# Copies of x's other half rows and stores issued by SP or ScalarE, some low parts on GpSimd, and new tables of order, banks and engines

## The chip, the cores and the metric

The kernel runs on one core of one Trainium2 chip. The metric is device time in microseconds (us) of one launch; lower is better. The engines are named as in the profile: PE is TensorE (PEld its weight loads), DVE is VectorE, ACT is ScalarE, POOL is GpSimd, SP is SyncE, which in the kernel before issues every DMA. "Banks" are the eight PSUM banks.

## The reference

Attention with 64-wide causal blocks over 8 batches, 8 heads, 576 rows and 64 columns a head, and then a mixing layer on its result. Cut to what matters:

```python
scores = (q @ k.transpose(0, 1, 3, 2)) / 8            # 8 batches, 8 heads, 576 x 576
scores = np.where(pos_i // 64 >= pos_j // 64, scores, -1e9)
attn = softmax(scores)                                # by rows
x = (attn @ v), heads side by side                    # 8 x 576 x 512, float32
theta = x @ w_theta
y = w_tok_r @ (x * cos(theta)) + w_tok_i @ (x * sin(theta))   # over the 576 rows
u = x + y
out = u + maximum(u @ w_ch, 0)
```

The four weights come in float64, the rest in float32.

## The kernel before, in words

**Products in halves.** Most matmuls take float16 operands that come in two: a high part (the value, scaled and rounded) and a low part (what the rounding left). A product is then three matmuls: high by high, low by high, high by low. The high part is made by a copy or a scaling, the low part by `value * scale - high`, which is one instruction on DVE (scalar_tensor_tensor) where a scale is needed. So `q_high`, `q_low`, `k_high`, `k_low`, `v_first`, `v_second` make the parts of a pair's q, k and v (`qh`, `ql`, `kh`, `kl`, `v1`, `v2`), `Weight.high_part` and `Weight.low_part` those of the weights, `high` and `low` those of the exponentials, `z_high` and `z_low` those of x times cosine and sine, `u_high` and `u_low` those of u. The start is different: batches 0 to 2 take q and k in float32, the first eight heads turn their exponentials on PE instead of by DMA, and the first four multiply them with v in float32.

**Attention.** A pair p is two heads. PE writes its scores into banks (`scores_wide`, `scores_narrow`, `scores_first`), DVE takes the largest of each row (`maxima`, tiles m), POOL or DVE makes of it the offset of the exponentials (`bias`, also on m), ACT the exponentials (`exponentials`, tiles t), then come their two parts (tile p) and a transposing DMA (`turn`, tile pt). PE multiplies them with v (`weighted`) into one bank o, and DVE divides by the row sums into the tile xn (`normalise`). The last 64 rows of a pair are spread over both halves of the partitions, so each head ends with a copy of 64 rows of 64 floats from one half of the partitions to the other, a DMA from xn to xn (`other_half`). The two parts of xn (tile xp) are turned by a second transposing DMA (`x_turn`, tile xT).

**Mixing.** PE makes theta from xT (`theta`), ACT and DVE reduce it to a turn between -1/2 and 1/2 (`turns`, `rest`, `size`), ACT makes sine and cosine (`sines`, with a load of ACT's function table ahead and behind), DVE and POOL multiply with x (`times_x`), and PE does the mixing over rows (`mix`) and the channel product (`channel`). ACT or DVE does the maximum (`rectify`), DVE the sum (`total`, into xT's buffer), and a DMA writes 128 x 576 floats of the result (`store`, xT to out, 32 in all).

**Order.** Nothing is scheduled at build time. The program consists of 3,444 parts (`add(key, f, needs, ...)`): `needs` are the parts that must stand earlier. Three tables fix the rest: ORDER is the order in which the parts are recorded, and so the order of each engine's queue; BANKS says which bank each product gets; PLACES names, for each part with an `on=` list, the engine that does it (A is ACT, D is DVE, P is POOL). `emit` walks through them:

```python
    for n in ORDER:
        key = keys[n]
        assert done.issuperset(parts[key].needs), key
        parts[key].f(*([place[key]] if parts[key].on else []))
```

Every engine runs its queue in order, and so does SP with its DMAs: a transfer whose data is late holds back every DMA recorded behind it. A DMA also waits until the one eight DMAs ahead of it has landed, since they share eight semaphores in turn. The two kinds of transfer that the change speaks of are added so:

```python
            add(("half", n), h.other_half, needs)                 # needs: normalise of head n
            part("store", (e,), m.store, [("out", b, e, th) for th in range(2)])
```

Of the kernel before, what the change touches and what calls it, by code (L numbers as in the profile page):

```python
# [21 lines left out]
ALU = mybir.AluOpType  # L22
# [17 lines left out]
    160, 158, 8, 0, 16, 9, 32, 40, 24, 10, 11, 334, 333, 1, 56, 339, 2, 338, 362, 363, 350, 17, 351, 3, 370, 18, 352,  # L40
    371, 48, 19, 33, 4, 353, 372, 20, 360, 41, 361, 335, 42, 354, 373, 12, 340, 336, 337, 364, 162, 374, 34, 382, 164,
    25, 365, 26, 383, 57, 5, 366, 386, 341, 58, 27, 59, 342, 367, 49, 13, 387, 72, 343, 104, 344, 64, 345, 50, 411,
    398, 368, 21, 347, 51, 43, 96, 346, 348, 35, 410, 381, 28, 80, 163, 36, 399, 408, 29, 88, 165, 409, 73, 166, 400,
    136, 105, 412, 167, 161, 74, 413, 401, 384, 168, 169, 388, 170, 414, 137, 65, 171, 172, 97, 332, 106, 418, 428,
    419, 415, 385, 81, 159, 420, 44, 138, 349, 107, 389, 178, 89, 98, 82, 99, 390, 355, 391, 83, 421, 90, 139, 6, 84,
    402, 120, 392, 91, 60, 356, 357, 52, 112, 482, 393, 358, 75, 422, 431, 432, 436, 359, 30, 380, 100, 375, 180, 66,
    37, 45, 22, 416, 53, 462, 92, 435, 67, 61, 23, 76, 68, 429, 113, 394, 483, 369, 69, 77, 449, 85, 121, 93, 101,
    437, 450, 463, 430, 114, 141, 376, 122, 142, 377, 14, 151, 378, 143, 451, 115, 433, 471, 108, 452, 453, 395, 434,
    396, 403, 460, 438, 461, 152, 472, 439, 397, 454, 440, 464, 182, 465, 123, 153, 466, 441, 442, 31, 404, 15, 473,
    379, 445, 467, 443, 176, 486, 446, 128, 405, 447, 468, 1804, 444, 474, 485, 469, 516, 540, 1805, 144, 129, 490,  # L50
    484, 183, 491, 406, 130, 407, 517, 181, 131, 489, 488, 525, 487, 423, 503, 504, 526, 505, 417, 514, 527, 492, 179,
    515, 493, 7, 506, 494, 475, 424, 518, 496, 519, 545, 425, 54, 507, 184, 426, 1806, 448, 455, 476, 520, 427, 55,
    508, 521, 177, 497, 456, 495, 457, 458, 132, 1807, 498, 459, 522, 523, 116, 539, 470, 46, 477, 528, 185, 499, 124,
    109, 70, 500, 1808, 478, 479, 102, 480, 543, 481, 501, 78, 544, 1809, 86, 117, 125, 554, 133, 509, 146, 502, 529,
    555, 38, 568, 567, 556, 173, 510, 94, 557, 530, 538, 576, 511, 1810, 512, 1811, 577, 62, 513, 531, 578, 541, 542,
    1812, 546, 524, 547, 558, 566, 1837, 532, 186, 1823, 565, 549, 533, 187, 569, 534, 548, 550, 188, 1838, 570, 1824,
    535, 571, 559, 551, 591, 572, 589, 1839, 71, 552, 1830, 140, 189, 573, 579, 596, 190, 536, 147, 1831, 593, 1832,
    1813, 592, 148, 597, 617, 642, 616, 587, 598, 599, 600, 620, 1814, 621, 590, 622, 174, 1815, 537, 595, 619, 580,
    1825, 560, 618, 574, 1816, 601, 627, 594, 39, 628, 154, 553, 605, 588, 1817, 606, 607, 145, 196, 629, 47, 608,
    1833, 1840, 581, 63, 1826, 1834, 609, 194, 1841, 1818, 602, 1835, 561, 1819, 1827, 1842, 1836, 1844, 647, 1843,  # L60
    1828, 1820, 603, 562, 563, 1829, 1821, 1845, 1846, 1847, 1848, 575, 1852, 640, 623, 1849, 79, 1850, 693, 582,
    1822, 624, 1866, 643, 1853, 1855, 583, 630, 631, 638, 95, 1854, 667, 644, 584, 1856, 668, 610, 648, 564, 1861,
    625, 639, 698, 1862, 632, 641, 1851, 585, 649, 669, 670, 1857, 1865, 671, 198, 650, 611, 103, 1873, 646, 1869,
# [1198 lines left out]
```

## Time and profile before

| | us |
|---|---|
| median of 3 runs (647.54 to 651.51) | 650.79 |
| the profiled execution | 651.37 |
| its span, first to last instruction | 649.6 |
| outside the span | 1.77 |
| PE busy / DVE / ACT / POOL | 621.8 / 568.0 / 509.4 / 364.4 |
| mean granted clock of PE, share of full | 0.992 |

A busy time is the union of an engine's instructions. Matmuls overlap in their pipeline, so a busy PE need not be a PE at its peak; what shows a loss for certain are its idle time and the stretches with a lower granted clock. Issuing a DMA does not count as busy.

### The profile page before, as it was taken

To read this page: it belongs to the slowest core of one execution; us is meant where nothing else is said; L and a number is where in the kernel's file an instruction comes from. 1 tells how busy PE (TensorE), PEld (TensorE's weight loads), DVE (VectorE), ACT (ScalarE), POOL (GpSimd) and SP (SyncE) were. 2 spreads that over 40 slices of the span, in tenths; PEclk is the share of its full clock that TensorE was granted. 3 is DMA by queue.
4 is the path that set the end of the run, shared out by engine and by line. 5 is a ranking of instruction groups with operands and counts; after the bars stand their busy time and mean duration, and the time that the engine had idled before them with its cause. 6 is when DMAs were issued, how large, how long until landed. Compare 5 with 4: busy or idle time off the path is not lost.

```text
span 649.6 us, 18112 instructions
## 1 busy us (share of the span) xinstructions
PE 621.8 (96%) x7412; PEld 465.8 (72%) x7414; DVE 568.0 (87%) x1141; ACT 509.4 (78%) x797; POOL 364.4 (56%) x404
## 2 busy tenths in 40 slices
PE   5699979999999999999999999999999999999997
PEld 3588657865886687866778667785776678857775
DVE  5999997998999989999989999999999998857653
ACT  5999898767997899888988989988997998218112
POOL 4345675655646389544665449574576466843530
PEclk9999996999999999999999999999999999999999
DMA  8964799978898788969779897988997647930001
GB/s 349 416 249 102 121 201 165 222 138 162 211 248 149 114 229 182 185 135 249 179 172 173 166 245 144 208 158 177 210 212 160 124 81 146 163 80 2 37 37 74
DMA packets 242403, 110.03 MB, mean 169 GB/s; under 512 B 229904, under 2 KB 229904, under 8 KB 242320
## 3 DMA queue, kind: packets, MB, share of 16 engines
q1 hardware_dynamic: 242320, 108.88, 74.8%
q8 instruction: 58, 0.95, 0.6%
q14 instruction: 25, 0.20, 0.1%
HBM read 42.01 MB, written 9.44 MB: 79 GB/s over the span
## 4 chain that ended last, share of the span: by engine, by line
PE 65%; ACT 13%; DMA 7%; DVE 7%; issue 4%; POOL 4%; SPq 0%; DVEq 0%; ACTq 0%; POOLq 0%
PE g L937 15%; PE s L937 9%; PE g L725 7%; PE g L861 6%; PE g L960 6%; PE s L597 5%; PE s L861 5%; ACT t L658 3%; PE s L960 3%; DMA pt<-in_w_tok 3%; PE g L597 2%; DMA pt<-p 2%; PE g L716 2%; ACT aa L904 1%; PE s L864 1%
## 5 line engine op out<-in xcount | busy, mean ns | idle before, releaser
L937 PEld LDWEIGHTS <-zh 128*128 128x128 f16 x1152 | 112.7, 98 | 30.6 <-issue 1.4
L937 PE MATMUL g<-wT_h,zh 128*128 128x288 f16 x369 | 105.6, 286 | 0.6 <-DVE xT L976 0.5
L937 PE MATMUL g<-wT_l,zh 128*128 128x288 f16 x369 | 105.5, 286 | 0.0
L937 PE MATMUL g<-wT_h,zl 128*128 128x288 f16 x369 | 105.5, 286 | 0.0
L725 PE MATMUL g<-v,pt 128*128 128x65 f16 x2700 | 93.5, 194 | 4.4 <-POOL rr L913 3.5
L725 PEld LDWEIGHTS <-pt 128*128 128x128 f16 x2700 | 89.9, 98 | 9.2 <-DMA pt<-p 4.9
L645 DVE TENSOR_REDUCE m<-s 128x1 f32<-128x448 f32 (+3 forms) x132 | 85.2, 674 | 6.6 <-PE s L604 6.4
L442 POOL TENSOR_TENSOR p<-t,p 128x1536 f16<-128x1536 f32 (+4 forms) x22 | 59.6, 2710 | 52.9 <-ACT p L437 33.7
L442 DVE TENSOR_TENSOR p<-t,p 128x1600 f16<-128x1600 f32 (+4 forms) x42 | 70.5, 1683 | 4.0 <-ACT p L437 2.5
L437 ACT CAST p<-t 128x1600 f16<-128x1600 f32 (+4 forms) x52 | 69.0, 1332 | 0.6
L937 PEld LDWEIGHTS <-zl 128*128 128x128 f16 x576 | 56.4, 98 | 17.3 <-issue 2.6
L658 ACT ACTIVATE t<-s,m,size 128x576 f32<-128x576 f32 (+1 forms) x80 | 60.2, 779 | 10.8 <-POOL m L653 9.4
L861 PEld LDWEIGHTS <-xT 128*128 128x128 f16 x384 | 35.5, 98 | 41.9 <-issue 3.8
L937 PE MATMUL s<-wT_h,zh 128*128 128x288 f16 x207 | 59.2, 286 | 1.9 <-ACT t L658 1.3
L937 PE MATMUL s<-wT_h,zl 128*128 128x288 f16 x207 | 59.2, 286 | 0.1
L937 PE MATMUL s<-wT_l,zh 128*128 128x288 f16 x207 | 59.2, 286 | 0.0
L960 PEld LDWEIGHTS <-wch_h 128*128 128x128 f16 x512 | 48.1, 98 | 14.2 <-issue 2.1
L645 DVE TENSOR_REDUCE m<-g 128x1 f32<-128x320 f32 (+2 forms) x156 | 54.1, 373 | 2.9 <-PE g L604 2.8
L913 POOL TENSOR_TENSOR rr<-rr,xn 128x256 f32<-128x256 f32 x38 | 36.6, 971 | 32.7 <-ACT rr L902 32.2
L658 ACT ACTIVATE t<-g,m,size 128x192 f32<-128x192 f32 (+2 forms) x100 | 49.6, 535 | 6.1 <-POOL m L653 5.2
L442 POOL TENSOR_TENSOR zl<-aa,zh 128x512 f16<-128x512 f32 (+1 forms) x34 | 39.9, 1180 | 19.6 <-ACT zh L437 17.6
L960 PE MATMUL g<-uh,wch_h 128*128 128x288 f16 x172 | 49.3, 286 | 0.3 <-DVE xT L976 0.3
(201 smaller groups left out, 1643.5 us busy)
## 6 DMA issues: line engine op xcount, KB each, us to landing
rv<-in_v SPq DMA_DIRECT2D x16, 768.0 KB, 5.3
rq<-in_q SPq DMA_DIRECT2D x16, 640.0 KB, 5.8
rk<-in_k SPq DMA_DIRECT2D x16, 576.0 KB, 4.9
out<-xT SPq DMA_DIRECT2D x32, 288.0 KB, 2.8
w_raw<-in_w_tok SPq DMA_DIRECT2D x5, 576.0 KB, 6.3
pt<-in_w_tok SPq DMA_DIRECT2D x4, 576.0 KB, 8.4
w_raw<-in_w_theta SPq DMA_DIRECT2D x4, 512.0 KB, 7.3
w_raw<-in_w_ch SPq DMA_DIRECT2D x4, 512.0 KB, 5.9
```

Of the source, the lines that this page charges most:

```text
L437: nc.scalar.copy(out=out, in_=x)
L442: engine_of(on).tensor_tensor(out=out, in0=x, in1=y, op=ALU.subtract)
L597: nc.tensor.matmul(to[hh][:, col:col + n], lhsT=qq[rows, P + P * i:P + P * i + P], rhs=kk[rows, k0:k0 + n], start=nn == 0 and col % 512 == ...
L645: nc.vector.tensor_reduce(out=self.m[:, i:i + 1], in_=self.scores_of(i), axis=AX.X, op=ALU.max)
L658: nc.scalar.activation(out=t_parts[self.hh][:, to:to + n], in_=self.scores_of(i), func=AF.Exp, scale=self.scales()[0], bias=self.m[:, NI + ...
L716: nc.tensor.matmul(o[:, i, :], lhsT=wide_of(source)[:, at_, :], rhs=v_wide[pair.p % 2][:, slot, hh, :], start=j == 0, stop=j == len(blocks ...
L725: nc.tensor.matmul(o[:, i, :], lhsT=source[:, block, :], rhs=vv[:, slot, hh, :], start=first, stop=last)
L861: nc.tensor.matmul(g, lhsT=xT[:, xx + i, :], rhs=ww[:, dt, :], start=first, stop=last)
L864: nc.tensor.matmul(g[half * D:half * D + D, 0:HC], lhsT=xT[:, xx + i, 0:D], rhs=ww[:, dt, half * HC:half * HC + HC], start=first, stop=last)
L913: engine_of(on).tensor_tensor(out=cd, in0=cd, in1=self.xns[dt][:, i0:i0 + ni, :], op=ALU.mult)
L937: nc.tensor.matmul(g, lhsT=zz[:, kk, cols], rhs=ww[:, kk, ts], start=(n == 0 and kk == k0 and nn == 0), stop=n == 4 and kk == k0 + ni - 1 ...
L960: nc.tensor.matmul(g[:, 0:HS], lhsT=ww[:, dt, e * P:(e + 1) * P], rhs=uu[:, dt, th * HS:(th + 1) * HS], start=dt == 0 and n == 0, stop=dt ...
```

## The change

It does four things. `other_half` and `store` take an engine: SP as before, or ACT. Six kinds of low part (`Weight.low_part`, `q_low`, `k_low`, `v_second`; the first counts for three weights) may now be done on POOL, in two steps: a scaling in place of the float32 value, then a subtraction. The parts that have an `on=` list are therefore more, and PLACES is longer. And all three tables hold new numbers: of the parts that PE runs, 313 of 957 stand at the same place in its queue as before, the others mostly a few places off.

Read against the parts, the new PLACES gives ACT 44 of the 64 half copies and 25 of the 32 stores; SP keeps 20 and 7. POOL gets 12 of the low parts: 5 `v_second`, 4 of weights, 2 `q_low`, 1 `k_low`. Of the parts that had a choice before, 281 change engines; in sum ACT gets 17 more high parts of x, z, q, v and u and 3 more of `size` and `rectify`, and loses 7 of the exponentials' high parts and the weights; three `low` of the exponentials and six `z_low` go from POOL to DVE, and ten `times_x` from DVE to POOL.

```diff
@@ -37,196 +37,198 @@
 ORDER = [
-    160, 158, 8, 0, 16, 9, 32, 40, 24, 10, 11, 334, 333, 1, 56, 339, 2, 338, 362, 363, 350, 17, 351, 3, 370, 18, 352,
...
 PLACES = (
-    "PDPDAPDDPPDPPDPPAAPAPPAAAAAPAADAPDAAPAPPAAAAAPAAPAADPADPAPAPDPDAAPDPADADPADDAPAPAPPAAPAPAPAAPDDPAPPAPPAPPPAPDAPP"
...
+    "PDPPDDPPADPDPDPPPAPDPAPDPAAPDAADDAADPAPDPAPDPAADDAPDPAADDAADPAADPAADDPADDASPADDSAPAADDADDDDSAPPADDAADADASDPPDADA"
...
+    def issuer(on):
+        return nc.scalar if on == "A" else nc.sync
...
+    def scaled_less(on, out, x, by, y):
+        if on == "D":
+            nc.vector.scalar_tensor_tensor(out=out, in0=x, scalar=by, in1=y, op0=ALU.mult, op1=ALU.subtract)
+        else:
+            scaled(on, x, x, by)
+            less(on, out, x, y)
...
-        def low_part(self):
-            nc.vector.scalar_tensor_tensor(out=self.lo, in0=self.val, scalar=self.up, in1=self.hi, op0=ALU.mult, op1=ALU.subtract)
+        def low_part(self, on):
+            scaled_less(on, self.lo, self.val, self.up, self.hi)
...
-        def other_half(self):
+        def other_half(self, on):
...
-            nc.sync.dma_start(out=x[other, NI - 1, mine], in_=x[mine, NI - 1, mine])
+            issuer(on).dma_start(out=x[other, NI - 1, mine], in_=x[mine, NI - 1, mine])
...
-        def store(self, e):
-            nc.sync.dma_start(out=out[self.b, e * P:(e + 1) * P, :], in_=self.result(e))
+        def store(self, e, on):
+            issuer(on).dma_start(out=out[self.b, e * P:(e + 1) * P, :], in_=self.result(e))
...
-            add(("half", n), h.other_half, needs)
+            add(("half", n), h.other_half, needs, on="SA")
...
-            part("store", (e,), m.store, [("out", b, e, th) for th in range(2)])
+            part("store", (e,), m.store, [("out", b, e, th) for th in range(2)], on="SA")
```

`q_low`, `k_low` and `v_second` change as `low_part` does. What the tables do is seen at three places. The names in the rows: w_raw and w_val are a weight's bits and its float32 value, t0 and t1 the exponentials of an even and an odd head, g4 to g7, s0 and s1 banks, m the offsets, pt the turned exponentials, rk, rq, rv the loaded k, q, v, xn the attention's result, junk a result that only its sum is wanted of. The change shifts the lines by 5 to 12, so that L477 before and L489 now are the same line; so are L429 and L434, L437 and L442, L658 and L667, L705 and L714, L731 and L740, L817 and L826, L823 and L832, L966 and L975, L980 and L989.

ACT at the start of the program, before: the conversions of the weights (L477) and the first exponentials of pair 0 (L658).

```order
L477 ACTIVATE w_val_139<-w_raw_137 128x512
L477 ACTIVATE w_val_139<-w_raw_136 128x512
L477 ACTIVATE w_val_139<-w_raw_138 128x512
L658 ACTIVATE t0_105<-g4_120,m_192 128x320
L658 ACTIVATE t0_105<-g4_120,m_192 128x192
L658 ACTIVATE t1_106<-g6_122,m_196 128x320
L477 ACTIVATE w_val_146<-pt01_115 128x576
L658 ACTIVATE t1_106<-g6_122,m_196 128x192
L477 ACTIVATE w_val_140<-pt11_116 128x576
L437 COPY pt00_113<-g4_120 128x512
L446 ACTIVATE wth_h_130<-w_val_139 128x512
L477 ACTIVATE w_val_139<-w_raw_138 128x512
```

The same place now:

```order
L489 ACTIVATE w_val_139<-w_raw_137 128x512
L489 ACTIVATE w_val_139<-w_raw_136 128x512
L489 ACTIVATE w_val_139<-w_raw_138 128x512
L495 ACTIVATE w_raw_138<-w_raw_138,eighth_83 128x512
L489 ACTIVATE w_val_146<-pt01_115 128x576
L667 ACTIVATE t0_105<-g5_121,m_183 128x320
L667 ACTIVATE t0_105<-g5_121,m_183 128x192
L667 ACTIVATE t1_106<-g6_122,m_188 128x320
L489 ACTIVATE w_val_140<-pt11_116 128x576
L667 ACTIVATE t1_106<-g6_122,m_188 128x192
L442 COPY pt00_113<-g5_121 128x512
L489 ACTIVATE w_val_139<-w_raw_138 128x512
```

The first exponentials now stand behind one more conversion (L495, which DVE did) and behind the fourth weight; the part with L446 has gone from ACT to DVE.

SP where the exponentials of heads 9 to 11 are turned (pt10, pt01, pt11), before:

```order
L705 DMA_TRANSPOSE pt10_114<-p1_109 128x16x128
L817 DMA rk_1147<-in_k 128x1152
L705 DMA_TRANSPOSE pt10_114<-p1_109 128x8x128
L817 DMA rq_1167<-in_q 128x1280
L705 DMA_TRANSPOSE pt01_115<-p0_108 128x18x128
L705 DMA_TRANSPOSE pt01_115<-p0_108 128x8x128
L731 DMA xn_1196<-xn_1196 64x64
L705 DMA_TRANSPOSE pt11_116<-p1_109 128x16x128
L705 DMA_TRANSPOSE pt11_116<-p1_109 128x8x128
L817 DMA rv_1327<-in_v 128x1536
L731 DMA xn_1196<-xn_1196 64x64
```

SP at the same place now:

```order
L714 DMA_TRANSPOSE pt10_114<-p1_109 128x16x128
L714 DMA_TRANSPOSE pt10_114<-p1_109 128x8x128
L826 DMA rv_1159<-in_v 128x1536
L714 DMA_TRANSPOSE pt01_115<-p0_108 128x8x128
L714 DMA_TRANSPOSE pt01_115<-p0_108 128x18x128
L714 DMA_TRANSPOSE pt11_116<-p1_109 128x16x128
L826 DMA rq_1298<-in_q 128x1280
L714 DMA_TRANSPOSE pt11_116<-p1_109 128x8x128
L826 DMA rk_1321<-in_k 128x1152
```

Ahead of head 10's transposes (pt01) stands one load (v) in place of two (k and q), the small transpose goes ahead of the large one, and the half copies have left for ACT's queue.

ACT between the exponentials of heads 37 and 38 (batch 4, the stores of batch 2), before:

```order
L429 ACTIVATE v10_87<-rv_3951,size_3359 128x12x64
L966 ACTIVATE g5_121<-g5_121,size_1146 128x288
L823 ACTIVATE junk_117,size_4681<-rk_4782 128x1152
L437 CAST p1_109<-t1_106 128x1536
L823 ACTIVATE junk_117,size_4681<-rk_4894 128x1152
L658 ACTIVATE t0_105<-s0_118,m_5083,size_3359 128x576
```

The same place now:

```order
L434 ACTIVATE v10_87<-rv_3965,size_3372 128x12x64
L667 ACTIVATE t1_106<-g4_120,m_4994,size_3372 128x192
L975 ACTIVATE g5_121<-g5_121,size_1158 128x288
L832 ACTIVATE junk_117,size_4475<-rk_4809 128x1152
L740 DMA xn_4815<-xn_4815 64x64
L989 DMA out_0<-xT_3128 128x576
L442 CAST p1_109<-t1_106 128x1536
L989 DMA out_0<-xT_3182 128x576
L832 ACTIVATE junk_117,size_4475<-rv_4675 128x1280
L667 ACTIVATE t0_105<-s0_118,m_5092,size_3372 128x576
```

One half copy and two stores stand on ACT's queue here, between the last exponential of head 37 and the first of head 38.

## Rows read from the trace of the kernel before

**Rows 1.** The page, part 1: busy us, share of the span, instructions.

```profile
PE 621.8 (96%) x7412; PEld 465.8 (72%) x7414; DVE 568.0 (87%) x1141; ACT 509.4 (78%) x797; POOL 364.4 (56%) x404
```

**Rows 2.** The page, part 4: the chain that ended last, shares of the span.

```profile
PE 65%; ACT 13%; DMA 7%; DVE 7%; issue 4%; POOL 4%; SPq 0%; DVEq 0%; ACTq 0%; POOLq 0%
```

**Rows 3.** Windows: stretch, its length, busy us of each engine, PE clock, DMA share.

```profile
6.58:36.00 29.42, 23.35 (x177) 17.86 (x179) 26.54 (x61) 26.41 (x47) 12.77 (x21) 1.00 1.00 408
...
92.60:97.30 4.70, 1.17 (x39) 1.20 (x40) 4.70 (x12) 4.62 (x7) 4.38 (x7) 1.00 0.90 177
97.30:107.60 10.30, 9.45 (x79) 6.93 (x77) 7.09 (x15) 9.04 (x18) 7.33 (x9) 0.51 0.92 180
107.60:195.00 87.40, 86.67 (x1037) 65.48 (x1034) 79.36 (x167) 69.00 (x115) 48.92 (x52) 1.00 0.96 193
195.00:553.00 358.00, 352.41 (x4613) 260.68 (x4613) 333.52 (x661) 319.70 (x477) 218.67 (x211) 1.00 0.82 172
```

**Rows 4.** Timeline of ACT, 7 to 17 us: start, us, what.

```profile
10.90 1.25 ACT L658 ACTIVATE t<-g,m 128x320 f32<-128x320 f32 x3
12.03 0.75 ACT L477 ACTIVATE w_val<-pt 128x576 f32<-128x576 f32 x1
...
14.30 0.63 ACT L446 ACTIVATE wth_h<-w_val 128x512 bf16<-128x512 f32 x1
```

**Rows 5.** Timeline of PE, 87 to 110 us; in brackets the idle time ahead.

```profile
88.35 2.17 PE L597 MATMUL s<-rk,rq 64*128 64x512 f32 x16
...
96.13 1.51 PE L725 MATMUL g<-v,pt 128*128 128x65 f16 x45 [3.55 <-POOL rr L913]
98.50 4.29 PE L597 MATMUL s<-rk,rq 64*128 64x512 f32 x13 [0.85 <-ACT t L658]
```

**Rows 6.** Timeline of SP, 79 to 99.5 us.

```profile
87.04 6.60 SPq L705 DMA_TRANSPOSE pt<-p  x2
93.75 0.52 SPq L731 DMA_DIRECT2D xn<-xn  x1
```

**Rows 7.** Timeline of ACT, 83 to 105 us.

```profile
90.28 0.61 ACT L446 ACTIVATE aa<-rr 128x512 f32<-128x512 f32 x1
...
97.18 2.42 ACT L658 ACTIVATE t<-s,m 128x576 f32<-128x576 f32 x4
```

**Rows 8.** By line, L731 and L980: ns min/median/max of one issue.

```profile
L731 SPq DMA_DIRECT2D xn<-xn x64: 461/472/1193, 34.2 to 571.2; - x64
L980 SPq DMA_DIRECT2D out<-xT x32: 332/480/680, 180.3 to 646.6; - x32
```

**Rows 9.** Waits of SP's queue: us in total, times, longest.

```profile
SPq L731 <- DVE xn L743: 26.5, 19, 3.4
```

**Rows 10.** Waits of PE, 195 to 553 us: the first and the last of nine.

```profile
PE s L937 <- ACT t L658: 1.3, 1, 1.3
...
PE g L725 <- DMA pt<-p: 0.2, 1, 0.2
```

**Rows 11.** Waits of ACT, 195 to 553 us: the first of eleven.

```profile
ACT t L658 <- POOL m L653: 14.6, 16, 2.3
```

**Rows 12.** Timeline of all engines, 331.5 to 334.2 us.

```profile
331.99 1.96 POOL L653 TENSOR_SCALAR m<-m,size 128x5 f32<-128x5 f32 x1 [0.88 <-DVE m L645]
332.14 1.75 DVE L442 TENSOR_TENSOR p<-t,p 128x1536 f16<-128x1536 f32 x1
...
333.98 0.83 ACT L658 ACTIVATE t<-s,m,size 128x576 f32<-128x576 f32 x1 [2.25 <-POOL m L653]
```

**Rows 13.** By line, L653, L581, L433, L442: ns min/median/max of one.

```profile
L653 POOL TENSOR_SCALAR m<-m,size x30: 269/346/1956, 204.8 to 545.2; 128x5 f32<-128x5 f32 x18, 128x4 f32<-128x4 f32 x12
...
L581 DVE SCALAR_TENSOR_TENSOR v<-rv,size,v x30: 1004/1017/1743, 38.1 to 561.7; 128x768 f16<-128x768 f32 x30
...
L433 POOL TENSOR_SCALAR v<-rv,size x6: 901/912/1398, 32.4 to 459.6; 128x768 f16<-128x768 f32 x6
...
L442 POOL TENSOR_TENSOR xp<-xn,xp x18: 1389/1406/2546, 50.4 to 561.1; 128x640 f16<-128x640 f32 x18
```

More of the change, by code (lines that the diff above doesn't have):

```diff
@@ new lines @@
+    "DDADPADSDAPSAADDADPDPAPADAPAPDADPAPSPAPAPPDDAPPDDADADADPAPDPAPDAAADDDAPPPAPPPADPPADDPAPDPAPDDAPDDAPDPAPPDADDADAD"
+    "ADAAAAAAAAAAAAAADAPADPDAADADDDAPPPAPPDPDDDAPDPAPPPADPDADPDADDPADDPADPADAPADAAAAAADAAASASPPAPDPADADDAADPDPPDPDPPA"
+    "PDDAPPPDDDDAPDPAPPDAPDDADPPADPADAPPDDADAAAAAAAAAAAPAPAPADDDAADPPPPPPAPDPADPDAPPDAPPPAPPPAPPPAPDPAPDPAPDAPADAPADA"
+    "DAAAADAAAAADAPAPADDADAAPPPDPPPPPPDPPPPPPPDPPDAPPPAPPPAPPPADPPAPDADADAPADDDAAADASAAAADAPAPAPADDDDPPPPPDADPDPPPPPD"
+    "PPADDDAPPDAPPDPDPDAPPPAPDADAPAPAADADAAAAAAAAAPADAPDDDDDDAPPPDPPAPDPADPPAPDPADPPPPPDPDPPADPPAPPDPDPAPAPDPPDADDDAA"
@@ L230 @@
+    "ASSAADPAPAPADDDDAADPAPPPAPDPPPPPADPPAPPDDDDDAPPPPPDPDPPDADDDDAPDDDADAAADAAASAS"
 )
@@ L578, in v_first, with v_second @@
             scaled(on, to[:, :, :, 0:D], self.raw("v"), self.mixer.scales["v"].up)
-        def v_second(self):
-            nc.vector.scalar_tensor_tensor(out=self.v2[:, :, :, 0:D], in0=self.raw("v"), scalar=self.mixer.scales["v"].up,
-                                           in1=self.v1[:, :, :, 0:D], op0=ALU.mult, op1=ALU.subtract)
+        def v_second(self, on):
+            scaled_less(on, self.v2[:, :, :, 0:D], self.raw("v"), self.mixer.scales["v"].up, self.v1[:, :, :, 0:D])
         def products(self):
@@ L1015, in attention_phase_mixer @@
         add(("w", n, 5), w.high_part, [("wa", n), ("wc", kind, 2)], on="ADP")
-        add(("w", n, 6), w.low_part, [("w", n, 5)])
+        add(("w", n, 6), w.low_part, [("w", n, 5)], on="DP")
     for kind in ("theta", "tok", "ch", "rows"):
@@ L1089, in attention_phase_mixer @@
             add(("kh", p), pair.k_high, [("vc", b, of, 2)] + turn_of("kh", s_last, QK_BUFS) + wide_last.pop(("kh", p % QK_BUFS), []), on="PAD")
-            add(("ql", p), pair.q_low, [("qh", p)] + turn_of("ql", s_last, QK_BUFS) + wide_last.pop(("ql", p % QK_BUFS), []))
-            add(("kl", p), pair.k_low, [("kh", p)] + turn_of("kl", s_last, QK_BUFS) + wide_last.pop(("kl", p % QK_BUFS), []))
+            add(("ql", p), pair.q_low, [("qh", p)] + turn_of("ql", s_last, QK_BUFS) + wide_last.pop(("ql", p % QK_BUFS), []), on="DP")
+            add(("kl", p), pair.k_low, [("kh", p)] + turn_of("kl", s_last, QK_BUFS) + wide_last.pop(("kl", p % QK_BUFS), []), on="DP")
             ready = [("ql", p), ("kl", p)]
@@ L1095, in attention_phase_mixer @@
         if 2 * p >= WIDE_HEADS:
-            add(("v2", p), pair.v_second, [("v1", p)])
+            add(("v2", p), pair.v_second, [("v1", p)], on="DP")
         wide = [("s1", p, hh, k) for hh in range(2) for k in range(2)]
```

29 lines of the change are left out of this document (11 added, 18 removed), and 346 rows, old and new, of the table ORDER.

## Prediction

> **What bounds the kernel now.** I read the page's busy times first. PE is busy 96% of the span, DVE 87%, ACT 78%, POOL 56% [rows 1], and the chain that ended last lies on PE for 65% and on ACT for 13% [rows 2]. So PE is the bound, and the question is how much of its time is lost at all. The windows answer that by stage [rows 3]. From 6.58 to 36 us PE is busy 23.35 of 29.42 us: 6.1 us are lost while the weights are converted and the first exponentials are made. From 92.6 to 97.3 it is busy 1.17 of 4.70, and in the 10.3 us behind, the granted clock is 0.51, the lower of its two levels (1.2 against 2.4 GHz); the clock fell right after PE had stood for 3.55 and 0.85 us [rows 5]. From 107.6 to 195 only 0.7 us are lost. From 195 to 553, more than half of the span, PE is busy 352.41 of 358 us: 5.6 us are lost, in nine kinds of wait of which the longest is 1.3 us and the one for transposing DMAs 0.2 us [rows 10]. There is little to be won anywhere else than in the first 108 us.
>
> Beside PE two engines are nearly full in that long stretch: DVE with 333.5 and ACT with 319.7 of 358 us [rows 3]. ACT has 38.3 us of idle time there, and its first wait, 14.6 us in 16 times, is for the offsets of the exponentials from POOL [rows 11].
>
> **The change part by part.** The sum is made against the profiled execution, 651.37 us, of which 1.77 lie outside the span; the median of the three runs, 650.79, is 0.58 lower.
>
> Start, +0.7 us. ACT's first exponentials start at 10.90 now [rows 4]. In the new order a conversion that DVE did and the fourth weight's (0.75 us, row at 12.03) stand ahead of them. They start later by up to about 1.5 us, but the work up to the end of this block is the same except for the added conversion, some 0.7 us by the weight conversion's row, and for the copy with L446 (0.63) which leaves ACT. So the lasting delay lies between 0.1 and 1.5 us; I take 0.7, since PE waits for ACT in this stretch anyway.
>
> The stop at 92.6 us, -0.6 us. The weighted product of head 10 stood until 96.13 [rows 5]. Its transposes were issued from 87.04 on, and the two together held SP for 6.60 us [rows 6]. Now one load instead of two is ahead of them and the small one goes first, so this wait should shrink. But next late is the wide score product at 98.50. It needs the four exponentials of heads 12 and 13, and ACT made them from 97.18 on in one piece of 2.42 us, to 99.60 [rows 7], at the end of an unbroken row of turns, table loads and sines that starts from theta. That row of work is the same now except for one `size` of 0.61 us [rows 7], which DVE takes over. So PE stands in the same place for the same reason, 0.6 us less, and I expect the clock to fall again. The half copy that ACT now issues here stands behind the four exponentials and costs the score product nothing.
>
> Copies and stores on ACT, 0 us. The trace of before has no DMA issue on ACT. The nearest rows are SP's own: 0.472 us for a half copy, 0.480 for a store in the median [rows 8], at most 1.19; at the lower end ACT might go on at once, at cost 0. I take 0.475, what the same issue costs SP. 69 issues make 32.8 us on ACT, of which I count 38, or 18.0 us, from 195 to 553. That leaves 20.3 of ACT's 38.3 idle us. They are hidden where ACT waits anyway: at 331.63 ACT stood for 2.25 us before the exponentials of head 38 [rows 12], and the three issues that the new order puts there take 1.4. Nearly all stand behind the point at which their data was ready before, by 2 to 15 us as the old trace has it, so that ACT should not wait inside them; where one does, the exponentials behind it wait too, and with them the banks that PE's next scores need. This cover is the weakest point, and its price is the second rival below.
>
> SP without them, 0 us. SP waited 26.5 us in 19 times for xn before issuing half copies [rows 9], with transposes queued behind. Those 19 waits go mostly, but PE waited for transposes only 0.2 us after 195 us [rows 10], so an earlier transpose finds nobody waiting.
>
> Low parts on POOL, 0 us. A `v_second` costs DVE 1.017 us; in two steps on POOL it is 0.912 for the scaling and, by the row of 640 columns (1.406) taken to 768, about 1.7 for the subtraction, 2.6 in all [rows 13]. Twelve such parts take about 11 us off DVE and put about 27 on POOL, which is idle for 44% of the span; the other moves give DVE about 8 us back and take some 28 from POOL (counts of parts by their median durations). So both end about where they were. Bounds: -2 us if DVE's 3 us less reach PE, +2 us if an offset waits behind a two-step part on POOL. What that would look like the trace shows: at 331.99 the offset of head 38 took 1.96 us on POOL in place of 0.35 in the median, while DVE ran a subtraction with two SBUF inputs for 1.75 us [rows 12, 13]. The Trainium skill says this is a rule (SBUF — State Buffer, section "Who interferes with whom"): such a DVE instruction contends with a GpSimd instruction that reads SBUF, and whichever comes second waits. By that rule the twelve subtractions on POOL, some 18 us, could each hold up DVE for as long, which would make DVE about 7 us fuller instead of emptier and the sum about 2 us worse; by the row the trace agrees on who is held up, and POOL was the one.
>
> Waits from 195 to 553 us, -2.8 us. The 5.6 us lost there hang on the order, and the order around them is new. The largest, 1.3 us behind head 36's product, keeps its place: the offset of head 38 still stands behind the same subtraction. Of the other 4.3 us I take two thirds. Bounds: all 5.6 gone, or twice as much lost.
>
> End: unchanged; the last product, maximum, sum and store still follow each other.
>
> Sum: +0.7 - 0.6 - 2.8 = -2.7, so 648.7 us by the profiled execution and **648.1 us** by the median.
>
> **The rivals.**
>
> The stop goes (faster). If the exponentials of heads 12 and 13 come early enough, PE doesn't stand at 92.6, and the clock stays at its upper level. Worth 3.5 us of idle time, 0.85 before the scores, and 4.7 us of clock: PE was busy 9.45 us at 0.51 [rows 3], work of about 4.8 at full clock. That is 9.0 instead of 0.6: 639.7 us. For it speaks that transposes and half copies no longer stand in one queue, against it ACT's unbroken row. It decides if the score product starts at most 1 us behind the second score product of the pair before.
>
> ACT becomes the bound (slower). 18 us of issues go into the 38.3 idle us of ACT from 195 to 553. Of these, 14.6 are waits for an offset [rows 11], directly ahead of exponentials that PE waits for. If half of the issues lie on that path instead of in its gaps, they cost 9.0 us: 657.1 us. It decides where the issues ahead of a tile's exponentials take longer than ACT's wait there, 2.25 us at most in the rows. For it speaks that ACT would be at 94% and DVE at 93% in one stretch, against it that the half copies and stores stand behind others' waits.
>
> Nothing is moved that counts. The transfers leave SP, but no transfer that anyone waits for is earlier, and the new order is as good as the old: 650 to 651 us. The Trainium skill has this as a rule (DMA: Bandwidth & Descriptors, section "Issuing engines are not separate DMA queues"): transfers started by different engines run on the same 16 DMA engines, and only the time to start them is saved. The row with 0.2 us of waiting agrees so far as it goes; by that rule alone the sum would be 0.
>
> **How the numbers follow.** Forecast 40%, its own range 643 to 654; nothing moved 13%; the stop goes 25%; ACT bounds 22%. A difference of under 1% (644.3 to 657.3 us) is about what a measurement of this kernel can't tell from no change. Faster by more than that: nearly all of the stop's 25% and 5 of the forecast, less 2: 28%. Slower: most of ACT's 22% and the forecast's upper end, 22%. Within: 50%. The range of 8 in 10 reaches from below the stop's 639.7 to a little above ACT's 657.1: 638 to 659.
>
> **What would show it.** Right: a stretch of about 10 us at half clock begins near 97 us again; the score product at about 98 waits for ACT; ACT's DMA issues take about 0.47 us each; PE's idle time from 195 to 553 is 2 to 5 us. Wrong: no stretch at half clock, or a second one; waits of PE for exponentials summing to over 8 us after 195 us; issues on ACT that take over 1 us, or hold it while data is on its way.

## The result, and the profile after

The changed kernel takes 657.97 us in the median of 6 runs (654.57 to 659.09), against 649.43 of the kernel before on the same chip (647.34 to 651.51, 6 runs): a ratio of 1.0123, interval 1.0087 to 1.016. The ratios here and below leave out executions that took over 1.5% more than the same kernel's fastest. It is slower by about 8 us where 3 us faster was forecast. Some 2.4 of these 8 us are probably clock and not the change: the six executions of the kernel before took 649.3 us in the mean, and 89 later ones 651.6, at a mean granted clock of 0.989 as the changed kernel's six. At equal clock the changed kernel is 5.6 us slower (table below). The profiled execution took 659.09 us, the longest of the six; its span is 657.3, 7.7 more than before.

The page of the changed kernel, part 1 (busy us, share of the span, instructions):

```profile
PE 622.2 (95%) x7414; PEld 464.8 (71%) x7414; DVE 568.0 (86%) x1138; ACT 514.4 (78%) x810; POOL 365.3 (56%) x406
```

But for 5 us on ACT no engine has over 1 us more work than in [rows 1], and PE has 0.4. So nearly all of the 7.7 us are waits of PE, and the windows of the changed kernel say in which stages (its counterparts of [rows 3], cut at the same places of the program; 369 to 380 is one stop and what follows it):

```profile
6.79:36.00 29.21, 23.24 (x175) 17.90 (x175) 26.91 (x62) 26.68 (x47) 9.85 (x14) 1.00 0.94 376
36.00:93.00 57.00, 55.14 (x643) 41.54 (x643) 53.48 (x127) 48.84 (x87) 40.40 (x47) 1.00 0.72 172
93.00:97.60 4.60, 1.53 (x18) 1.23 (x19) 4.60 (x11) 4.48 (x7) 3.70 (x6) 0.86 1.05 236
97.60:106.00 8.40, 7.97 (x70) 5.79 (x71) 7.03 (x18) 7.79 (x15) 6.42 (x8) 0.50 0.63 148
106.00:195.00 89.00, 86.57 (x1069) 65.67 (x1068) 80.83 (x167) 75.95 (x125) 42.51 (x45) 1.00 0.98 190
195.00:369.00 174.00, 170.71 (x2232) 127.83 (x2231) 159.45 (x322) 153.91 (x233) 93.29 (x98) 1.00 0.82 176
369.00:380.00 11.00, 8.22 (x39) 3.96 (x37) 10.40 (x13) 8.04 (x12) 4.65 (x4) 0.84 0.78 131
380.00:558.00 178.00, 173.53 (x2325) 128.74 (x2324) 165.24 (x326) 158.89 (x241) 113.63 (x111) 1.00 0.82 166
558.00:657.30 99.30, 95.24 (x865) 72.09 (x861) 59.48 (x101) 28.52 (x47) 48.01 (x46) 0.99 0.28 68
```

Of the same stages before, two are not among [rows 3]:

```profile
36.00:92.60 56.60, 56.27 (x654) 43.82 (x654) 54.31 (x125) 52.09 (x91) 28.74 (x37) 1.00 0.69 156
553.00:649.60 96.60, 92.54 (x827) 69.82 (x824) 61.89 (x104) 27.27 (x47) 40.75 (x39) 1.00 0.28 66
```

Length less PE's busy time is PE's loss, and read against these and [rows 3] it comes to this. Start: 5.97 us for 6.07. From 36 us to the stop: 1.86 for 0.33. The stop: 3.07 and 0.43 for 3.53 and 0.85, with the clock at its lower level behind it again. Up to 195: 2.43 for 0.73. From 195 to 558: 3.29, 2.78 and 4.47, in sum 10.5, for 5.6, and a second, short stretch at the lower clock. End: 4.06 for 4.06. The three growing stages give 1.5, 1.7 and 4.9 us, 8.1 in all. Only the stop got better by more than 0.1 us, by 0.9.

In the first of the growing stages it is one wait, 1.61 us before 79.69 for exponentials of ACT; in the second two, 1.17 us before 144.24 for turned exponentials and 0.86 before 146.63 for ACT. The five largest waits of PE from 195 to 558 us, in the changed kernel (us in total, times, longest); before, the first was 1.3 us [rows 10]:

```profile
PE g L870 <- DVE u L955: 2.8, 1, 2.8
PE g L606 <- DVE xT L985: 1.6, 1, 1.6
PE s L946 <- ACT t L667: 1.3, 1, 1.3
PE s L870 <- ACT t L667: 1.3, 2, 1.0
PE s L382 <- POOL diag L376: 1.2, 1, 1.2
```

The longest in the timeline, all engines, 369 to 375 us; in brackets the idle time ahead:

```profile
369.61 3.10 POOL L447 TENSOR_TENSOR p<-t,p 128x1536 f16<-128x1536 f32 x1
...
369.98 3.41 DVE L447 TENSOR_TENSOR xp<-xn,xp 128x640 f16<-128x640 f32 x1 [0.60 <-ACT xp L442]
...
374.51 0.50 DVE L955 SCALAR_TENSOR_TENSOR u<-g,size_tok,u 128x288 f32<-128x288 f32 x1
...
375.07 0.38 PE L870 MATMUL g<-wth_h,xT 128*128 128x512 f16 x1 [2.77 <-DVE u L955]
```

DVE's low part of x takes 0.81 us elsewhere (138.69 in this trace). Here it starts 0.4 us behind POOL's low part of head 41, which reads SBUF as it does, and ends 0.7 us behind it: 2.6 us lost on DVE, and the sum u that frees PE's bank stands behind it. In the order before, the two parts were on the other engines (head 41 on DVE, x on POOL) and did not meet.

A second kind, POOL held up by DVE, in the timeline at 268 us:

```profile
267.80 2.63 POOL L376 TENSOR_SCALAR diag<-ident_r,size 128x128 bf16<-128x128 f32 x3
268.00 1.84 DVE L447 TENSOR_TENSOR p<-t,p 128x1600 f16<-128x1600 f32 x1
...
270.49 0.32 PE L382 MATMUL s<-diag,ones 128*128 128x384 bf16 x1 [1.19 <-POOL diag L376]
```

Three diagonals take 0.38 us each where DVE is not in the way (68.85 in this trace); the second of these took 1.94. The Trainium skill (SBUF — State Buffer, section "Who interferes with whom") says that a DVE instruction with two SBUF inputs contends with a GpSimd instruction that reads SBUF, that the lock is exclusive, and that the order of issue decides who waits. The two fences agree with it, on both sides: 3.41 us on DVE in place of 0.81, 1.94 on POOL in place of 0.38. The stop that both kernels have, head 38's offset at 331.99 [rows 12], does not agree by the letter: POOL's start is recorded 0.15 us ahead of DVE's, and POOL was the one that waited; POOL's starts are rough.

The stop at 94.5 us, PE and the instruction that released it:

```profile
97.02 0.47 DVE L752 TENSOR_TENSOR xn<-g,r 128x320 f32<-128x320 f32 x1
...
97.54 2.63 PE L734 MATMUL g<-v,pt 128*128 128x65 f16 x45 [3.07 <-DVE xn L752]
...
100.61 1.22 PE L606 MATMUL s<-rk,rq 64*128 64x512 f32 x2 [0.43 <-ACT t L667]
```

And ACT with the issues that it has got, at three places (ACTq is an issue):

```profile
129.11 0.73 ACT L442 CAST xp<-xn 128x640 f16<-128x640 f32 x1 [2.73 <-DMA xn<-xn]
129.12 0.47 ACTq L740 DMA_DIRECT2D xn<-xn  x1
129.74 0.72 ACT L434 ACTIVATE wch_h<-w_val,size_ch 128x512 f16<-128x512 f32 x1
...
179.75 2.22 ACTq L989 DMA_DIRECT2D out<-xT  x1
...
206.37 0.47 ACTq L740 DMA_DIRECT2D xn<-xn  x1
206.88 0.83 ACT L667 ACTIVATE t<-s,m,size 128x576 f32<-128x576 f32 x1 [0.41 <-issue]
```

The first is the usual case: the issue runs beside the conversion that stands ahead of it in ACT's queue, and the next instruction follows without a gap. In the third ACT had nothing else under way and stood for 0.41 us. Of the 35.5 us of the 69 issues, 28.4 lie beside an instruction of ACT, added up over the trace, and 7.1 beside none, 2.9 of these in the end behind 558 us; 52 of the issues are covered for over nine tenths of their length.

Last, one line of the waits of SP's queue:

```profile
SPq L860 <- DMA out<-xT: 14.0, 5, 4.3
```

The transpose of x (L860) writes into the buffer in which an earlier result still lies, and waits until that result's store has landed: five times, 14.0 us in all. Before it waited once, for 0.6.

### The profile page after: what moved, and what is told of

Read it like the earlier page. It is cut to its first block, busy times and chain, and to the rows that moved or that the text cites. A ratio compares the mean times of both kernels' runs of the same rounds, so it can differ in the third digit from the quotient of the medians.

```text
span 657.3 us, 18105 instructions
## 1 busy us (share of the span) xinstructions
PE 622.2 (95%) x7414; PEld 464.8 (71%) x7414; DVE 568.0 (86%) x1138; ACT 514.4 (78%) x810; POOL 365.3 (56%) x406
## 4 chain that ended last, share of the span: by engine, by line
PE 53%; ACT 21%; DVE 10%; DMA 7%; issue 5%; POOL 3%; ACTq 0%; SPq 0%; POOLq 0%; DVEq 0%
PE g L946 9%; PE s L946 8%; ACT t L667 7%; PE g L734 6%; PE g L969 5%; PE g L870 5%; PE s L870 5%; PE s L969 4%; PE s L606 4%; DMA xn<-xn 3%; DVE m L654 3%; ACT p L442 3%; ACT aa L913 3%; PE g L606 2%; PE g L725 2%
## 5 line engine op out<-in xcount | busy, mean ns | idle before, releaser
L654 DVE TENSOR_REDUCE m<-s 128x1 f32<-128x576 f32 (+3 forms) x132 | 85.4, 672 | 5.4 <-PE s L613 5.3
L447 DVE TENSOR_TENSOR p<-t,p 128x1600 f16<-128x1600 f32 (+4 forms) x45 | 76.7, 1705 | 3.5 <-ACT p L442 3.2
L447 POOL TENSOR_TENSOR p<-t,p 128x1536 f16<-128x1536 f32 (+4 forms) x19 | 48.0, 2530 | 40.5 <-ACT p L442 33.8
L442 ACT CAST p<-t 128x1536 f16<-128x1536 f32 (+4 forms) x50 | 66.9, 1343 | 3.2 <-DMA pt<-p 1.8
L667 ACT ACTIVATE t<-s,m,size 128x576 f32<-128x576 f32 (+1 forms) x80 | 59.9, 781 | 7.4 <-POOL m L662 6.1
L922 POOL TENSOR_TENSOR aa<-aa,xn 128x256 f32<-128x256 f32 (+1 forms) x64 | 47.5, 754 | 19.5 <-ACT aa L913 18.3
L667 ACT ACTIVATE t<-g,m,size 128x320 f32<-128x320 f32 (+2 forms) x100 | 49.3, 535 | 5.7 <-POOL m L662 5.7
L969 PE MATMUL g<-uh,wch_l 128*128 128x288 f16 x168 | 48.0, 286 | 0.0
```

The costliest lines, as they stand in the source:

```text
L442: nc.scalar.copy(out=out, in_=x)
L447: engine_of(on).tensor_tensor(out=out, in0=x, in1=y, op=ALU.subtract)
L654: nc.vector.tensor_reduce(out=self.m[:, i:i + 1], in_=self.scores_of(i), axis=AX.X, op=ALU.max)
L667: nc.scalar.activation(out=t_parts[self.hh][:, to:to + n], in_=self.scores_of(i), func=AF.Exp, scale=self.scales()[0], bias=self.m[:, NI + ...
L922: engine_of(on).tensor_tensor(out=cd, in0=cd, in1=self.xns[dt][:, i0:i0 + ni, :], op=ALU.mult)
L969: nc.tensor.matmul(g[:, 0:HS], lhsT=ww[:, dt, e * P:(e + 1) * P], rhs=uu[:, dt, th * HS:(th + 1) * HS], start=dt == 0 and n == 0, stop=dt ...
```

## The experiments

Thirteen kernels, in the order in which they ran. The first four shared a chip, and so did the second four and the last five; each ratio is against the kernel before, run on that chip beside them. The last column removes one disturbance. How many stretches at half clock an execution gets differs from run to run, in the kernel before too: 89 executions of it, run beside the experiments, took 648.21 us in the mean at a mean granted clock of 0.997 (12 of them) and 654.57 at 0.981 (10), and lie within 0.6 us (standard deviation) of a line that falls by 3.8 us for each 0.01 of clock. The column is the mean distance of a kernel's runs above that line, with its standard error. It leaves out what a kernel's own stops cost it in clock, and it takes the line to hold on every chip.

| kernel | ratio to before | interval | us above before at equal clock |
|---|---|---|---|
| the changed kernel | 1.0123 | 1.0087 to 1.016 | 5.6 ± 0.6 |
| 1 after, all transfers on SP | 1.0236 | 1.0192 to 1.0279 | 12.9 ± 1.0 |
| 2 after, low parts on DVE | 1.0236 | 1.0195 to 1.0278 | 13.7 ± 1.0 |
| 3 before, transfers on ACT | 1.0079 | 1.0042 to 1.0116 | 4.9 ± 0.4 |
| 4 before, low parts on POOL | 1.0019 | 0.999 to 1.0049 | 0.3 ± 0.2 |
| 5 after, one stop mended | 1.0111 | 1.0075 to 1.0148 | 7.3 ± 0.6 |
| 6 after, six stops mended | 1.0049 | 1.0021 to 1.0077 | 3.3 ± 0.5 |
| 7 after, division earlier | 1.0127 | 1.0082 to 1.0172 | 8.6 ± 1.3 |
| 8 after, 44 issues more | 1.0248 | 1.0202 to 1.0295 | 16.3 ± 0.9 |
| 9 before, stores on ACT | 1.0067 | 1.0037 to 1.0098 | 4.8 ± 0.3 |
| 10 before, half copies on ACT | 0.9999 | 0.9967 to 1.0031 | 0.8 ± 0.3 |
| 11 before, offset of head 38 on DVE | 0.9967 | 0.9936 to 0.9998 | -0.8 ± 0.2 |
| 12 after, stores on SP | 1.0077 | 1.0042 to 1.0112 | 5.6 ± 0.6 |
| 13 after, six stops mended, stores on SP | 1.004 | 1.0009 to 1.0072 | 1.8 ± 0.4 |

In the edits below a letter in brackets is the engine of a part (S is SP), and parts stand in the order of recording.

**1 to 4: the features by themselves.** The theory was that the loss sits in the order; its rivals put it on ACT's issues and on the two-step low parts.

```diff
 (1, in after)
-half: A x44, S x20; store: A x25, S x7
+half: S x64; store: S x32
 (2, in after)
-v_second x5, weights x4, q_low x2, k_low x1: [P]
+the same twelve: [D]
 (3, in before)
-half: S x64; store: S x32
+half: A x44, S x20; store: A x25, S x7
 (4, in before)
-the twelve low parts: [D]
+the same twelve: [P]
```

> The changed kernel, its order, banks and all other engines as they are, with all 64 half copies and 32 stores issued by SP. Theory (the order): the loss lies where the new tables put instructions of DVE and POOL side by side that hold each other up, or queue a late instruction ahead of one that PE waits for; who issues the copies and stores costs nothing. Then it takes 654 to 661 us, like the changed kernel's 657.97. Rival 1 (the issues): ACT loses the time of its 69 issues on the path; then it falls to 649 to 652 us.

> The changed kernel with its 12 low parts back on DVE in one step, everything else as it is. Theory (the order): 655 to 660 us, as before this edit. Rival 2 (the two-step low parts): their 27 us on POOL and what they do to DVE are the loss; then 649 to 652 us.

> The kernel before, in its own order, with the same 44 half copies and 25 stores issued by ACT. Theory (the order): 647 to 652 us, as the kernel before. Rival 1 (the issues): 655 to 660 us, ACT with some 29 us of issues more on its queue.

> The kernel before, in its own order, with the same 12 low parts on POOL in two steps. Theory (the order): 647 to 653 us. Rival 2 (the two-step low parts): 655 to 660 us.

Only the fourth went as the theory said: the two-step low parts cost nothing in the old order. The third did not: the issuers cost 0.8% there. The first two fit neither side. Undoing either feature in the new order doubles the loss, so the features are not what is too much in it. The reading that fits is that the order is fitted to them, and that parts which are put back meet others at the wrong time; it was not tested part by part. In the second the new waits are for turned exponentials, 5.3 us in 3 times, where after has 1.2 in one. The stops at 94 to 96 (3.07 us), 269 to 276 (1.2), 337 to 343 (1.3) and 546 to 554 us (1.6) stand in both as long as they do in after, to within 0.02 us: they owe nothing to who issues a transfer or to the low parts.

**5 and 6: the stops.**

```diff
 (5)
 [P]mn.42 [A]xh.4.3 [D]xl.4.3
-[P]low.41
 e.42.3 ... u.3.3.0 m.43.1 [P]mn.43
+[P]low.41 turn.41
 (6: the edit of 5, and)
-[P]mn.38 [P]mn.50
+[D]mn.38 [D]mn.50
-[D]low.30 ... vm.4 ... vc.4
+vm.4 ... vc.4 [D]low.30 turn.30
-[D]z.6.0.4.0 ... [A]relu.5.0.0 out.5.0.0
+[A]relu.5.0.0 out.5.0.0 [D]z.6.0.4.0
-[D]w.8.6 ... [D]mn.10 m.11.2 m.11.3
+[D]mn.10 m.11.2 m.11.3 [D]w.8.6
-[P]xh.1.3 ... [P]mn.18
+[P]mn.18 [P]xh.1.3
```

(w.8.6 is the low part of a weight, xh and xl are the parts of x, mn an offset, vm, vc the size of v, whose diagonals are vb.)

> The changed kernel with one part moved: the low part of head 41 on POOL stands behind the offset of head 43, so that it no longer runs beside DVE's low part of x (3.41 us in place of 0.81 in the profile after). Theory (the order): PE's stop of 2.77 us at 375 shrinks to under 1 us and the 3.4 us at half clock behind it go; 652 to 656 us. Rival (ACT is the bound, so that what is saved here is lost to the next exponentials): 657 to 659 us, with as much idle time of PE between 195 and 558 us as the changed kernel's 10.5.

> The changed kernel with the cause of six stops taken away, issuers and two-step low parts as they are: four parts moved behind what they held up (low part of head 41 on POOL, low part of head 30 on DVE, one product with x on DVE, one weight's low part on DVE), the fourth high part of x of batch 1 on POOL behind the offset of head 18, and the offsets of heads 38 and 50 on DVE in place of POOL. In the profile after, the six cost PE 2.8, 1.2, 1.6, 1.6, 0.9 and 2.4 us and 1.7 of clock, 12 in all. Theory (the order): 647 to 651 us if no new stop of over 1 us comes. Rival (ACT is the bound): 655 to 659 us, other stops in their place.

Six stops mended bring the loss from 1.23% to 0.49%, at equal clock from 5.6 ± 0.6 to 3.3 ± 0.5 us, the surer number, since the kernel before took 651.7 us in the mean beside run 6 and 649.3 beside the changed kernel. One of the six, the offset of head 38, stands in the kernel before too, and mending it there gives 0.8 us (run 11). The one stop alone brings nothing that the times show (7.3 against 5.6 us at equal clock, the wrong way). The trace of 5 says why: the stop of 2.77 us is gone, and three of 0.83, 0.30 and 0.90 us stand between 370 and 381 in its place, 2.0 in sum, the first and the last for exponentials of ACT. PE loses 10.3 us from 195 to 558 where after loses 10.5, so for this one stop the rival's picture came: 658.88 us, and what was saved there was lost again behind it. That of the six comes back in part; a window of 6:

```profile
195.00:553.00 358.00, 351.19 (x4601) 259.46 (x4599) 335.50 (x661) 321.93 (x489) 210.76 (x211) 1.00 0.85 172
```

PE loses 6.8 us where after has 10.5 and before 5.6, and ACT still has 36 us of idle time: it is the next to be late in places, but not full. New stops stand at 87 (1.15) and 195 us (1.14). The time, 655.83 us beside a kernel before of 652.84, lies in the rival's range (655 to 659) and not in the theory's (647 to 651); but of the rival's picture only a part is true, since the stops did not come back elsewhere in full.

**7: what is next late at 94 us.** The prediction put the wait there on transposes, and ACT's exponentials next.

```diff
-normalise.9.0 normalise.9.1 ... [D]w ... [D]v2.6 ... normalise.9.2
+normalise.9.0 normalise.9.1 normalise.9.2 ... [D]w ... [D]v2.6
```

> The changed kernel with the division of head 9 put ahead of three instructions of DVE, which held it back until 97.02 us. Theory of the prediction (behind this wait the exponentials of heads 12 and 13 on ACT are next late): the weighted product of head 10 starts 1 to 2 us earlier, the score product behind it waits as much longer, the stretch at half clock stays; 656 to 660 us. Rival (the stop is DVE's alone): the stop of 3.07 us shrinks to about 1, no stretch at half clock near 100 us; 650 to 654 us.

PE and ACT of this kernel, 94 to 101 us:

```profile
94.74 1.53 PE L743 MATMUL g<-v,pt 128*128 128x65 f16 x45
...
98.47 0.74 ACT L676 ACTIVATE t<-s,m 128x576 f32<-128x576 f32 x1
...
100.94 1.22 PE L615 MATMUL s<-rk,rq 64*128 64x512 f32 x2 [4.67 <-ACT t L676]
```

The product that stood for 3.07 us stands no more, so its exponentials had long been turned. The score product starts at 100.94 for 100.61: the whole wait has moved to ACT, whose exponentials begin at 98.47, behind the sines and the load of the function table. A stretch at half clock follows. The time, 1.0127 as a ratio and 661.08 us in the median, is no better than that of after and just above the 656 to 660 expected: taking DVE's wait away gained nothing.

**8: the price of an issue.**

```diff
             issuer(on).dma_start(out=x[other, NI - 1, mine], in_=x[mine, NI - 1, mine])
+            if on == "A":
+                nc.scalar.dma_start(out=spare[other], in_=ident[mine, 0:D])
```

> The changed kernel with 44 issues more on ACT: behind each half copy of ACT a second, idle copy of 64 x 64 floats from a constant to a spare tile. Rival 1 (an issue takes ACT's time, 0.47 us each): 20 us more on ACT, of which half or more reaches PE; 664 to 672 us. Theory (an issue runs beside ACT's own instruction and costs it nothing): 656 to 661 us.

667 us: rival 1's number. How the time was lost the trace shows better than the sum. The timeline of ACT near 209 us, at the place that was quoted of after at 206:

```profile
208.84 0.47 ACTq L741 DMA_DIRECT2D xn<-xn  x1
209.35 0.86 ACTq L743 DMA_DIRECT2D spare<-ident_r  x1
210.26 0.83 ACT L668 ACTIVATE t<-s,m,size 128x576 f32<-128x576 f32 x1 [1.31 <-issue]
```

One issue stood ACT for 0.41 us there, two for 1.31, and PE's next stop is 1.37 us (0.32 in after). Two issues in a row can't both run beside the one instruction ahead of them: of 113 issues' 73.3 us, 24.1 lie beside nothing, against 7.1 of 35.5 in after, so the 44 more cost ACT 17 us. So an issue costs ACT what the instruction ahead of it does not cover. The 69 issues of the change, most of them apart, leave 7 us of ACT beside nothing in the whole span; from 195 to 558 us only 0.4 us of its idle time are ended by an issue. So run 8 prices a pair of issues and not a lone one. The 44 added transfers also run on the DMA engines, which was not taken apart, and take their turns of the eight semaphores, which held up next to nothing: three issues began within 0.3 us of the landing that freed theirs, in after none.

**9 and 10: which transfer it is.** Run 3 is taken apart.

```diff
 (9, in before)
-store: S x32
+store: A x25, S x7
 (10, in before)
-half: S x64
+half: A x44, S x20
```

> The kernel before, in its own order, with 25 stores issued by ACT and all half copies by SP. Theory (a store on ACT no longer stands behind the transposes in SP's queue, starts beside them, and they land later): most of the 0.8% of the third run, a ratio of 1.004 to 1.008, and a wait of PE for turned exponentials of about 1.4 us near 354 us. Rival (it is ACT's time in the issues, 0.34 us for a store against 0.47 for a half copy, a quarter of the sum): 0.999 to 1.003.

> The kernel before, in its own order, with 44 half copies issued by ACT and all stores by SP. Theory (the stores' transfers beside the transposes are what costs): a ratio of 0.998 to 1.003, no wait for turned exponentials near 354 us. Rival (ACT's time in the issues): three quarters of the 0.8%, 1.004 to 1.008.

The stores, as the theory said: 1.0067 against 0.9999, though the half copies are two thirds of ACT's issue time (21.0 us in run 10, 9.6 for the stores in run 9). The waits of PE for turned exponentials from 107 to 553 us rise from 0.8 us in the kernel before to this:

```profile
PE g L743 <- DMA pt<-p: 4.2, 5, 1.5
```

The three long ones end at 204, 361 and 486 us (1.54, 0.99, 0.94). The way to the first can be followed. SP's waits from 185 to 200 us:

```profile
SPq L869 <- DMA out<-xT: 4.5, 1, 4.5
```

The timelines of ACT and of SP there:

```profile
186.52 0.38 ACTq L998 DMA_DIRECT2D out<-xT  x1
```

```profile
194.79 1.33 SPq L869 DMA_TRANSPOSE xT<-xp  x1
196.22 9.27 SPq L723 DMA_TRANSPOSE pt<-p  x2
```

A transpose of x (L869) must wait until the store of the result that lies in its buffer has landed. ACT issues this store at 186.52, beside loads of q, k and v, and it lands 8.2 us later (2.8 us is the median of a store before, 4.0 here). SP stands for 4.5 us until then, the transposes of the exponentials stand behind it in its queue, and PE waits for these. So the theory named the right transfers, and for this wait the wrong way: it is not that the store starts beside transposes, but that it lands late, and that SP's queue waits for it. For the wait at 361 us it may be as the theory has it: two stores are issued inside the second of two transposes, which holds SP for 4.14 in place of 3.66 us. The third is not explained, and of the 4.8 us at equal clock these waits are 3.5. The Trainium skill (DMA: Bandwidth & Descriptors, section "Issuing engines are not separate DMA queues") says that transfers of all issuers share the same engines; the trace agrees so far as it goes: the store of ACT, issued among SP's loads, took 8.2 us to land where 2.8 is usual.

**11: the stop that both kernels have.**

```diff
-[P]mn.38
+[D]mn.38
```

> The kernel before with one part on another engine: the offset of head 38 on DVE, ahead of the subtraction beside which it took 1.96 us on POOL. Theory (POOL and DVE hold each other up): the stop of 1.34 us at 334 goes or shrinks to under 0.6 us, nothing else changes; 0.997 to 1.000. Rival (the exponentials behind it are late for another reason): the stop stays above 1 us, 0.999 to 1.002.

All engines of this kernel near 330 us, the place of [rows 12]:

```profile
329.64 0.22 DVE L671 TENSOR_SCALAR m<-m,size 128x5 f32<-128x5 f32 x1
329.77 1.74 DVE L456 TENSOR_TENSOR p<-t,p 128x1536 f16<-128x1536 f32 x1
329.95 1.45 ACT L676 ACTIVATE t<-s,m,size 128x576 f32<-128x576 f32 x2 [1.53 <-DVE m L671]
...
331.45 0.28 PE L955 MATMUL s<-wT_h,zh 128*128 128x288 f16 x1 [0.64 <-ACT t L676]
```

The offset takes 0.22 us ahead of the subtraction instead of 1.96 beside it, and the stop falls from 1.34 to 0.64 us (under 0.6 was expected). At equal clock the kernel is 0.8 ± 0.2 us faster than before, the 0.7 that the stop gave up: it beats both kernels, if by little (0.9967).

**12 and 13: are the stores the rest?**

```diff
 (12, in after; 13, in the kernel of 6)
-store: A x25, S x7
+store: S x32
```

> The changed kernel with all 32 stores issued by SP, half copies as they are. Theory (a store on ACT starts beside transposes that SP's queue would put ahead of it, 0.7% in the old order): the same here, a ratio of 1.003 to 1.009 in place of 1.012. Rival (the new order is fitted to where its transfers start, so that every one that is put back costs): 1.012 to 1.024, as with all of them on SP.

> The kernel with six stops taken away (1.005), with all 32 stores issued by SP as well. Theory (stops and stores add up to the whole loss): 0.996 to 1.001. Rival (fitted order): 1.005 to 1.015.

By the ratio 12 is half way back, inside the theory's range, but the intervals of 12 and after overlap, and at equal clock 12 is where after is, 5.6 us, with most of the stops of after in its trace. So no price of the stores shows in the new order, as it shows in the old; after waits for turned exponentials only 1.2 us in all, 12 for 0.8. 13 is at 1.8 ± 0.4 us against 3.3 ± 0.5 of 6, and by the ratio, which lies in neither range, they are the same. What the two leave open stands below.

## Why the prediction was wrong

**The sign.** The step that failed is "Waits from 195 to 553 us, -2.8". It took the new order to be better than the old by two thirds of 4.3 us, for no other reason than that it was new. In its place PE lost 4.9 us more there, and two stages that had no term in the sum (36 to 92.6 and 107.6 to 195, 0.33 and 0.7 us before) another 1.5 and 1.7. Six mended stops, with all of the features left in, take 2.3 ± 0.8 us off at equal clock, of 5.6 (run 6; 0.74% by the ratios): that much is shown to be order, less the 0.8 us of head 38's offset, which the old order loses too. The bound "twice as much lost" held the size, but its sign was a guess that no row supported. The sign of being wrong that was named for it came too: a second stretch at half clock, behind the stop of 2.77 us.

**How such a stop comes about.** Named for "Low parts on POOL", and right about the rule: DVE and POOL hold each other up. But I asked it of the twelve new low parts, and these cost 0.3 ± 0.2 us in the old order (run 4). It was the parts that had always had a choice, 281 of them moved, that met: head 41's low part went to POOL and x's to DVE, and the sum behind them made PE stand for 2.77 us. I had also read [rows 12, 13] as "POOL was the one" that is held up; at 369.98 it is DVE, at 268 POOL.

**Copies and stores on ACT, 0 us.** The price of 0.475 us was right (468 ns for a half copy in the median, 342 for a store), and so was next to nothing on the path, for a reason that I did not have: an issue runs beside the instruction ahead of it. "18.0 us" of ACT's idle time were never taken: ACT's idle time that an issue ended is 0.4 us from 195 us on, and its waits for offsets are 11.8 where they were 14.6 [rows 11]. The second rival (ACT becomes the bound) gave 657.1, and the time came within 1 us of it, and so inside the stated range, by another mechanism: ACT is idle for 42 of 363 us from 195 to 558. That is luck. (The 2.25 us of ACT's wait in [rows 12] begin at 331.73, not at 331.63.)

The same step says of the transfers that they "stand behind the point at which their data was ready before, by 2 to 15 us", and took that for harmless to ACT. Who waits for a store that comes late was not asked. It is the transpose of x, into the same buffer. In the old order the stores on ACT cost 4.8 us (run 9), of which one wait of 1.54 us was followed back to such a transpose.

**SP without them, 0 us.** Half of it held: the half copies' leaving costs or gives 0.8 us at most (run 10). With the stores SP's queue lost something too: a store that it issued itself had nearly always landed when the next transpose of x came (0.6 us of waiting, once). In the new order no such price shows in the time (run 12), although SP's wait for stores falls from 14.0 to 6.2 us there; so the stores are no proved part of the 8 us.

**The stop at 92.6 us, -0.6, and the clock.** Near in size (4.4 to 3.5 us) and right in what is next late (run 7). Wrong in what ends it: not the transposes of [rows 6], which had landed at 95.51, but the division of head 9 on DVE, which ended at 95.99 in the kernel before, 0.14 us ahead of the product in [rows 5], and at 97.49 here. The row of before:

```profile
95.51 0.48 DVE L743 TENSOR_TENSOR xn<-g,r 128x320 f32<-128x320 f32 x1
```

(The releaser that [rows 5] names, rr on POOL, ended at 96.04 and is no operand of the product.) The stretch at half clock came again, as forecast. It began at 97.6 in the kernel before, ahead of the 0.85 us of the second stop and not behind them, and at 96.3 here, within the first.

**Start, +0.7.** PE's first product began 0.2 us later with its load, and the stage lost 5.97 us for 6.07: the lower bound of 0.1 was the place.

**What stays open.** After six mended stops 3.3 ± 0.5 us are left at equal clock, with the stores back on SP 1.8 ± 0.4. New stops of about 1 us and many short waits stand in their traces, but which of them hold the 3.3 us was not shown. Nor was it shown why runs of the new order scatter by 1.3 to 2.8 us (standard deviation) about the line of equal clock, where those of the old scatter by 0.6. And run 5 against run 6 leaves unexplained which of the six stops pays.

## What to carry to other kernels

When a change rewrites the order, price the order apart from the features: put each feature alone into the old order, and take each alone out of the new. Here the new order lost another 1.1% with either feature taken back, and the old one 0.8% with the transfers given to ACT, so neither direction alone is evidence against a feature. Nor does every part cost: 25 stores given back to SP changed nothing at equal clock (run 12).

Before a store is given to another, fuller queue, ask who writes its buffer next: a store that lands late holds up that writer, and everything queued behind the writer (4.5 us on SP's queue in run 9, at one place). Look for stops where a two-input subtraction on DVE stands beside work of POOL that reads SBUF, and move the one that someone waits for: a 0.2 us instruction put ahead of it is the cheapest mend in this study.

## What the runs showed of the hardware

An issue on ACT runs beside ACT's own instruction: 28.4 of 35.5 us were covered. It shows where ACT has nothing else under way (0.41 us at 206), and most where two stand in a row (1.31 us in run 8). Beside transposes on SP an issue of ACT can take 2.22 us in place of 0.34: the one quoted at 179.75 ended at 181.96, SP's transposes at 181.82. Of the 39 issues that began beside transposes, 33 took under 0.6 us.

How much of a run PE spends at half clock differs between executions of one program: those of the kernel before had a mean granted clock of 0.981 to 0.997, worth 6.4 us. A difference of 1% between two kernels of this size is not read well without the clock of each run beside its time.
